# Decoding float64 weights in two VectorE passes instead of four, with one pass more on GpSimd, and chunks two slots earlier

## The chip, the cores and the metric

One core of a Trainium2 chip runs the whole program in one launch. The metric is device time in microseconds, from launch to end; a lower time is better. The profile records one execution of the program, engine by engine.

## The reference

Three layers follow each other: an attention with a threshold, a first feed-forward mixture with a rational activation, and a second mixture of 8 experts with one expert per token. The part that matters here is the middle one, which takes 2304 tokens of width 512 to width 2048 and back:

```python
h = x @ w_in                      # (2304, 512) @ (512, 2048)
P = a[0] + a[1] * h + a[2] * h2 + a[3] * h3
Q = 1.0 + np.abs(b[0]) * np.abs(h) + np.abs(b[1]) * h2
g = P / (Q + 1e-06)
return (g @ w_out).astype(np.float32)
```

`w_in` and `w_out` arrive as float64, because a float32 draw is multiplied by a float64 factor. A weight is thus two 32-bit words, and the kernel makes a float32 of them on the chip: the sign and exponent and the upper 20 bits of the mantissa sit in the high word, three more mantissa bits at the top of the low word. Everything later works with a constant power of two that the scale factors remove.

## The kernel before

**Stages.** The attention runs in steps of one 128-row tile, 144 of them, with a tail of 12 more steps in which only the products with V (L429, "PV" below) and the transposes of the result (L221) are left. A second program, `moe1`, is a generator that the attention loop advances once per step from step 112 on. Its unit is the *slot*: slot 32 is the step after the last score tile, slot 43 is the attention's last step, and from slot 44 on `moe1` runs alone. Each engine works through its instructions in the order in which these two programs wrote them.

**Weights come in 32 pieces** of 128x512 weights (16 of `w_in`, 16 of `w_out`), in the order of `STREAM`. A piece is loaded into one of 5 `raw` buffers by a DMA on the SP queue, and the next load is issued when a piece is finished (`load_next`). Decoding a piece takes five instructions. ScalarE writes the absolute value of the high word, read as a float32 (L609, `mag`). VectorE then clamps it (L612), shifts it left by 3 and masks it (L616), ORs in the low word shifted right by 29 (L620) and ORs in the sign (L625). For the first 8 pieces the intermediate `mag` lies in SBUF, and a table of costs (`RATES`, `decode_steps`) spreads their four passes one by one over slots 32 to 45. For the other 24 it lies in one PSUM bank (`acc`, `aux`), and all four passes of a piece stand in one slot: one piece every 1.6 slots, from slot 47 on.

**After decoding**, a `w_in` piece is summed (L767, ScalarE; for pieces 0 to 3 the sum over partitions is a small matmul L776 of its own on TensorE), scaled (L810; piece (0,2) on GpSimd, L808) and split into two float16 halves, `wih` (L811, ScalarE) and `wil` (L812, GpSimd). A `w_out` piece is split in L817 (ScalarE) and L818 (GpSimd).

**Chunks.** The first mixture's work is 96 chunks, one per slot, of 128 hidden units by 384 tokens, from slot `START` = 43 on. Chunk c has 12 matmuls L893 (`emit_in`), and chunk c-5 has its 9 matmuls L963 in the same slot (`emit_out`). Two chunks share one PSUM tile `h`, and there are two such tiles; a *pair* is two chunks. For each pair the activation is a chain across engines. ScalarE: L917, L918, L919. GpSimd: L920. VectorE: L922, L923. ScalarE: logarithm and exponential, L929 and L930, which overwrite `h`. VectorE: L908, L909, L910, the last reader of `h`. Then L944 (ScalarE) and L945 (GpSimd) split the result. In a slot with the second chunk of a pair, VectorE's order is L908, L909, L910 of the pair before, then the decoding passes of that slot, then L922, L923. In the other slots the decoding passes stand between L923 and L908.

## Time and profile before

| | |
|---|---|
| median of 3 runs | 1044.03 us (1043.01 to 1044.04) |
| the profiled execution | 1049.4 us, span 1047.7 us |
| TensorE busy | 940.3 us, 90% |
| VectorE busy | 832.6 us, 79% |
| ScalarE busy | 688.6 us, 66% |
| GpSimd busy | 502.2 us, 48% |
| granted TensorE clock, mean | 0.971 of full speed |

The shares are averages over stages with different limits. The attention ends about 325 us into the span, the chunks of the first mixture run from there to about 784 us, and decoding goes on until 532 us. In the tables, PE is TensorE, PEld its weight loads, DVE VectorE, ACT ScalarE, POOL GpSimd and SP the queue that issues most DMAs; L12 is line 12 of the kernel before.

### The profile page before, as it was taken

Reading aid. Unit: us, or ns where it says so; the run is one execution under the profiler, and the core shown is the slowest. Engines: PE = TensorE matmul, PEld = TensorE weight load, DVE = VectorE, ACT = ScalarE, POOL = GpSimd, SP = SyncE. Lnnn points to the kernel's source line nnn. Section 1 sums busy time; section 2 is a strip of 40 time slices with the busy share of each in tenths; the row PEclk is TensorE's granted clock in tenths of the full one; section 3 lists DMA queues with packets and bytes.
Section 4 is the critical chain, followed back from the end, with each engine's and each line's share of the span. In section 5 each row is a group of like instructions: output and inputs, shape, how many; then the busy total and the mean of one; then the engine's idle time right before and its main releaser. Section 6 shows DMA issues by size and latency. Waiting matters only on the chain. (4 is left out here: it accounts for less than half of the span.)

```text
span 1047.7 us, 20733 instructions
## 1 busy us (share of the span) xinstructions
PE 940.3 (90%) x7899; PEld 686.8 (66%) x7899; DVE 832.6 (79%) x1381; ACT 688.6 (66%) x1017; POOL 502.2 (48%) x485
## 2 busy tenths in 40 slices
PE   8898899999965887977989989998888999999996
PEld 5565566666553555655656666665557899999995
DVE  5887799999996799999868788898984896665552
ACT  5887788888864787786766666665563555555552
POOL 2687789888943546354454444442533022111120
PEclk9999999999986999999999999999999999999998
DMA  9999999999992134133001131214122111111350
GB/s 213 171 206 200 196 190 184 202 182 196 223 204 85 57 101 131 61 97 105 1 1 61 31 91 41 51 41 131 51 61 101 41 50 63 41 41 41 101 142 23
DMA packets 234187, 110.25 MB, mean 105 GB/s; under 512 B 196832, under 2 KB 221408, under 8 KB 234080
## 3 DMA queue, kind: packets, MB, share of 16 engines
q1 hardware_dynamic: 230816, 98.89, 43.7%
q0 software_dynamic: 3120, 9.96, 3.0%
q8 instruction: 64, 1.05, 0.4%
q14 instruction: 43, 0.35, 0.1%
q10 hardware_dynamic: 144, 0.00, 0.0%
HBM read 82.61 MB, written 13.63 MB: 92 GB/s over the span
## 5 line engine op out<-in xcount | busy, mean ns | idle before, releaser
L893 PE MATMUL h<-xT,wih 128*128 128x384 f16 x768 | 194.9, 337 | 48.9 <-DVE s L910 33.3
L401 POOL TENSOR_TENSOR php<-e,php 128x512 f16<-128x512 f32 x144 | 166.3, 1159 | 65.6 <-ACT php L399 61.8
L920 POOL TENSOR_TENSOR t<-t,ah 128x768 f32<-128x768 f32 x48 | 87.7, 1826 | 228.4 <-ACT t L919 213.8
L893 PEld LDWEIGHTS <-wih 128*128 128x128 f16 x768 | 69.8, 100 | 115.8 <-DVE s L910 40.4
L963 PE MATMUL acc<-woh,gh 128*128 128x512 f32 x288 | 126.4, 439 | 4.5 <-ACT part L980 2.0
L893 PE MATMUL h<-xT,wil 128*128 128x384 f16 x384 | 128.9, 336 | 0.5 <-POOL wil L812 0.5
L383 ACT ACTIVATE e<-s,mn 128x576 f32<-128x576 f32 x144 | 107.1, 743 | 30.7 <-DVE mn L382 26.5
L371 PE MATMUL s<-kt,qT 64*128 64x256 f32 (+3 forms) x640 | 117.0, 456 | 5.9 <-DVE mn L388 5.6
L395 DVE SCALAR_TENSOR_TENSOR e<-s,mn,e 128x576 f32<-128x576 f32 x144 | 116.4, 808 | 5.8 <-ACT e L383 5.8
L429 PEld LDWEIGHTS <-pt 128*128 128x128 f16 (+1 forms) x2240 | 80.5, 102 | 57.3 <-issue 54.0
L963 PE MATMUL acc<-wol,gh 128*128 128x512 f32 x288 | 114.6, 398 | 2.6 <-POOL wol L818 2.6
L963 PE MATMUL acc<-woh,gl 128*128 128x512 f32 x288 | 114.4, 397 | 0.0
L382 DVE TENSOR_REDUCE mn<-s 128x1 f32<-128x576 f32 x144 | 107.8, 748 | 7.0 <-PE s L371 6.9
L1659 POOL DMA_INDIRECT out_dram<-os,sidx x19 | 24.5, 1288 | 184.6 <-ACT os L1658 153.9
L399 ACT ACTIVATE php<-e 128x576 f16<-128x576 f32 x144 | 98.6, 685 | 9.6 <-DMA pt<-php 8.0
L429 PE MATMUL xps<-vs__112,pt 128*128 128x65 f16 (+1 forms) x2240 | 94.8, 197 | 0.0
L945 POOL TENSOR_TENSOR gl<-s,gh 128x768 fp32r<-128x768 f32 x48 | 91.2, 1900 | 6.9 <-issue 4.7
L929 ACT ACTIVATE h<-t,co 128x768 f32<-128x768 f32 x48 | 43.4, 904 | 57.0 <-DVE s L923 21.3
L917 ACT ACTIVATE ah<-h,cvs 128x768 f32<-128x768 f32 x48 | 43.2, 900 | 52.8 <-PE h L893 49.6
L963 PEld LDWEIGHTS acc<-woh,gh 128*128 128x128 f32 x288 | 54.8, 190 | 21.1 <-ACT part L980 4.9
L1592 DVE TENSOR_TENSOR wol<-xT,woh 128x1024 fp32r<-128x1024 f32 x45 | 56.8, 1270 | 14.6 <-ACT woh L1591 14.3
L908 DVE SCALAR_TENSOR_TENSOR t<-t,co,h 128x768 f32<-128x768 f32 x48 | 48.5, 1009 | 24.8 <-ACT h L930 13.4
(382 smaller groups left out, 2320.2 us busy)
## 6 DMA issues: line engine op xcount, KB each, us to landing
xT<-in_moe_w_dram SPq DMA_DIRECT2D x80, 512.0 KB
raw<-in_moe_w_in_dram SPq DMA_DIRECT2D x16, 512.0 KB
raw<-in_moe_w_out_dram SPq DMA_DIRECT2D x16, 512.0 KB
yd<-y SPq DMA_DIRECT2D x18, 256.0 KB
raw<-in_k_dram SPq DMA_DIRECT2D x16, 256.0 KB
raw<-in_q_dram SPq DMA_DIRECT2D x16, 256.0 KB
xT<-in_v_dram SPq DMA_DIRECT2D x8, 512.0 KB
part<-part SPq DMA_DIRECT2D x15, 256.0 KB
```

The costliest lines, as they stand in the source:

```text
L371: nc.tensor.matmul(ps[po:po + m, o:o + n], qT[r, g % 2, hh, t, po:po + m], KT[g][r, bb, c:c + n], start=True, stop=True)
L382: nc.vector.tensor_reduce(mn[:, n:n + 1], st[i], axis=AX.X, op=ALU.min)
L383: nc.scalar.activation(e[:, n], st[i], AF.Exp, bias=mn[:, n:n + 1], scale=-1.0)
L395: nc.vector.scalar_tensor_tensor(e[:, n], st.pop(i), mn[:, 2 + n:3 + n], e[:, n], op0=ALU.is_le, op1=ALU.mult)
L399: nc.scalar.activation(hi, e[:, n], AF.Copy)
L401: nc.gpsimd.tensor_tensor(lo[:, b:b + 512], e[:, n, a:a + 512], hi[:, a:a + 512], op=ALU.subtract)
L429: nc.tensor.matmul(x, pt[:, blk, po:po + m], vv[:, par, hh, j, :], start=False, stop=(i % 6 == 5 and n == 13))
L893: nc.tensor.matmul(hb[:, 0:n], w[:, k, fc * P:(fc + 1) * P], xT[:, k, t0:t0 + TR, lo, :], start=(i == 0), stop=(i == 11))
L920: nc.gpsimd.tensor_tensor(t1, t1, ah, op=ALU.mult)
L945: nc.gpsimd.tensor_tensor(gl, s, gh.bitcast(F32), op=ALU.subtract)
L963: nc.tensor.matmul(acc[r, i], g[:, i * P:(i + 1) * P], w, start=first and m == 0, stop=last and m == 2)
L1592: (self.nc.gpsimd if pool else self.nc.vector).tensor_tensor(cut(lo), src, cut(hi).bitcast(F32), op=ALU.subtract)
```

## The change

A piece is decoded by four instructions now, two of them on VectorE. GpSimd rewrites the low word in place (`last_bits`): it reads the words as unsigned integers, multiplies by 2^-29 and limits to 7.25, which leaves the word's top three bits as a small integer. ScalarE multiplies the high word, read as float32, by 2^-112 instead of taking its absolute value (`exponent`). VectorE shifts that left by 3 and ORs in the low word's three bits (`merge`), then ORs in the sign (`sign`). The clamp and the mask are gone.

```diff
-END = 46
-START = 43
+END = 44
+START = 41
-RATES = ((32, 1050), (42, 1150))
-FIRST_PIECES = 8
-DEC_AT = 47
+FIRST_AT = (32, 33, 35, 37, 38, 40, 42, 43)
+SHIFT_AT = (24, 25, 26, 27, 28)
+SHIFT_LEAD = 3
+DEC_AT = 45
 DEC_EVERY = 1.6
...
-    def mag(self, raw, t):
-        self.nc.scalar.activation(t, raw.bitcast(F32)[:, :, 1], AF.Abs)
-    def clamp(self, t, pool=False):
-        (self.nc.gpsimd if pool else self.nc.vector).tensor_scalar(t, t, HI_BITS, LO_BITS, op0=ALU.min, op1=ALU.max)
-    def shift(self, t):
-        t = t.bitcast(I32)
-        self.nc.vector.tensor_scalar(t, t, 3, 0x3FFFFFF8, op0=ALU.logical_shift_left, op1=ALU.bitwise_and)
-    def low(self, raw, t):
+    def last_bits(self, raw):
+        x = raw.bitcast(U32)[:, :, 0]
+        self.nc.gpsimd.tensor_scalar(x, x, 2.0**-29, 7.25, op0=ALU.mult, op1=ALU.min)
+    def exponent(self, raw, t):
+        self.nc.scalar.activation(t, raw.bitcast(F32)[:, :, 1], AF.Copy, scale=SHORTER)
+    def merge(self, raw, t):
         t = t.bitcast(I32)
         self.nc.vector.scalar_tensor_tensor(
-            t, raw[:, :, 0], 29, t, op0=ALU.logical_shift_right, op1=ALU.bitwise_or)
+            t, t, 3, raw[:, :, 0], op0=ALU.logical_shift_left, op1=ALU.bitwise_or)
...
-    begin, end = plan_decode()
-    for key, i, t in decode_steps():
-        steps.setdefault(t, []).append(lambda key=key, i=i: step(key, i))
-    for key in STREAM:
-        at(begin[key] - (MAG_LEAD if key in STREAM[:FIRST_PIECES] else 1), mag, key)
+    end = decode_at()
+    for n, key in enumerate(STREAM):
+        t = end[key]
+        steps.setdefault(t, []).append(lambda key=key: step(key))
+        at(t - (MAG_LEAD if n < len(FIRST_AT) else 1), exponent, key)
+        at(SHIFT_AT[n] if n < len(SHIFT_AT) else t - (MAG_LEAD if n < len(FIRST_AT) else SHIFT_LEAD), last_bits, key)
```

The first 8 pieces are now decoded in the slots of `FIRST_AT`, the last of them in slot 43 instead of 45. Chunks begin in slot 41 instead of 43, so that chunks 0, 1 and 2 are written among the attention's last three steps; the decoding of the other 24 pieces keeps its distance to the chunks, as does everything that is counted from `START`. GpSimd's new pass stands in slots 24 to 28 for pieces 0 to 4, two slots ahead of the VectorE passes for pieces 5 to 7, and three ahead for the rest.

**VectorE, among chunks 2 to 6**, from the L922 and L923 of the second pair. Before (L908 to L910 and L922, L923 are the activation, L612 to L625 the decoding):

```order
L922 SCALAR_TENSOR_TENSOR s<-s,cvs,h 128x768
L923 SCALAR_TENSOR_TENSOR s<-s,cvs,h 128x768
L612 TENSOR_SCALAR acc<-acc 128x512
L616 TENSOR_SCALAR acc<-acc 128x512
L620 SCALAR_TENSOR_TENSOR acc<-raw,acc 128x512
L625 SCALAR_TENSOR_TENSOR mag<-raw,acc 128x512
L908 SCALAR_TENSOR_TENSOR t<-t,co,h 128x768
L909 SCALAR_TENSOR_TENSOR h<-t,h 128x2x384
L910 SCALAR_TENSOR_TENSOR s<-s,co,h 128x768
```

and now (L892, L893 are the former L922, L923; L878 to L880 the former L908 to L910; L598 is `merge` and L603 `sign`):

```order
L892 SCALAR_TENSOR_TENSOR s<-s,cvs,h 128x768
L893 SCALAR_TENSOR_TENSOR s<-s,cvs,h 128x768
L598 SCALAR_TENSOR_TENSOR acc<-acc,raw 128x512
L603 SCALAR_TENSOR_TENSOR mag<-raw,acc 128x512
L878 SCALAR_TENSOR_TENSOR t<-t,co,h 128x768
L879 SCALAR_TENSOR_TENSOR h<-t,h 128x2x384
L880 SCALAR_TENSOR_TENSOR s<-s,co,h 128x768
```

Two of the four passes between L923 and L908 are gone; the same holds between L910 and L922 in the other kind of slot.

**GpSimd, from the attention's last tiles to the second pair of chunks.** Before (L401 and L407 are the attention's, the others as above):

```order
L401 TENSOR_TENSOR php<-e,php 128x512 x2
L407 TENSOR_TENSOR php<-e,php 128x2x64
L812 TENSOR_TENSOR wil<-mag,wih 128x4x128 x2
L920 TENSOR_TENSOR t<-t,ah 128x768
L808 TENSOR_SCALAR mag<-mag,sc 128x512
L812 TENSOR_TENSOR wil<-mag,wih 128x4x128 x2
L920 TENSOR_TENSOR t<-t,ah 128x768
```

and now (L591 is `last_bits`; L382, L388 the former L401, L407; L783 the former L812, L890 L920, L779 L808):

```order
L591 TENSOR_SCALAR raw<-raw 128x512
L382 TENSOR_TENSOR php<-e,php 128x512 x2
L388 TENSOR_TENSOR php<-e,php 128x2x64
L382 TENSOR_TENSOR php<-e,php 128x512 x2
L388 TENSOR_TENSOR php<-e,php 128x2x64
L783 TENSOR_TENSOR wil<-mag,wih 128x4x128 x2
L591 TENSOR_SCALAR raw<-raw 128x512 x3
L890 TENSOR_TENSOR t<-t,ah 128x768
L591 TENSOR_SCALAR raw<-raw 128x512
L779 TENSOR_SCALAR mag<-mag,sc 128x512
L783 TENSOR_TENSOR wil<-mag,wih 128x4x128 x2
L591 TENSOR_SCALAR raw<-raw 128x512
```

The first row is the fifth `last_bits`; four others stand among the four L382 and two L388 just ahead of it, and one now stands between L920 and L808.

**ScalarE, around the first pair of chunks.** Before (L457 copies a transposed attention result out of PSUM):

```order
L457 ACTIVATE xT<-tp 128x3x128 x2
L917 ACTIVATE ah<-h,cvs 128x768
L918 ACTIVATE s<-h,co,cvs 128x768
L919 ACTIVATE t<-ah,co 128x768
L811 ACTIVATE wih<-mag 128x4x128
L810 ACTIVATE mag<-mag,sc 128x512
L811 ACTIVATE wih<-mag 128x4x128
L929 ACTIVATE h<-t,co 128x2x384
```

and now (L887 to L889 are the former L917 to L919, L782 and L781 the former L811 and L810, L438 the former L457, L899 the former L929):

```order
L887 ACTIVATE ah<-h,cvs 128x768
L888 ACTIVATE s<-h,co,cvs 128x768
L889 ACTIVATE t<-ah,co 128x768
L782 ACTIVATE wih<-mag 128x4x128
L781 ACTIVATE mag<-mag,sc 128x512
L782 ACTIVATE wih<-mag 128x4x128
L438 ACTIVATE xT<-tp 128x3x128 x2
L899 ACTIVATE h<-t,co 128x2x384
```

The last two L457 of the attention moved from ahead of the first pair's activation to behind it and behind the splits of pieces (0,2) and (0,3). On TensorE chunk 0 stands ahead of the last two PV steps now, chunk 1 ahead of the last one, and chunk 2 behind the last transposes.

## Rows read from the trace of the kernel before

**Rows 1.** Busy time in two stretches; columns: stretch, length, each engine, clock, DMA.

```profile
420.19:428.31 8.12, 8.12 (x44) 5.51 (x43) 7.47 (x9) 5.84 (x9) 3.13 (x2) 1.00 0.24 67
354.41:524.46 170.05, 145.98 (x728) 96.17 (x727) 155.53 (x231) 127.84 (x185) 86.30 (x55) 0.98 0.25 79
```

**Rows 2.** TensorE's waits from 354.41 to 524.46: us in total, times, longest.

```profile
PE h L893 <- DVE s L910: 19.5, 12, 3.4
PE acc L963 <- ACT part L980: 2.0, 3, 1.0
PE acc L963 <- DVE part L980: 1.5, 2, 1.4
```

**Rows 3.** VectorE's groups from 354.41 to 524.46: count, busy us, mean ns, idle before.

```profile
L612 DVE TENSOR_SCALAR acc<-acc 128x512 f32<-128x512 f32 x22 | 15.2, 693 | 0.2
L616 DVE TENSOR_SCALAR acc<-acc 128x512 int32<-128x512 int32 x21 | 14.7, 699 | 0.7
```

**Rows 4.** VectorE in order of time: start, duration, instruction, idle before it.

```profile
354.05 0.69 DVE L612 TENSOR_SCALAR acc<-acc 128x512 f32<-128x512 f32 x1
...
356.85 1.01 DVE L922 SCALAR_TENSOR_TENSOR s<-s,cvs,h 128x768 f32<-128x768 f32 x1
...
360.83 1.01 DVE L908 SCALAR_TENSOR_TENSOR t<-t,co,h 128x768 f32<-128x768 f32 x1 [1.93 <-ACT h L930]
...
363.81 0.69 DVE L612 TENSOR_SCALAR acc<-acc 128x512 f32<-128x512 f32 x1
```

**Rows 5.** GpSimd's groups over the whole run, shapes apart.

```profile
L945 POOL TENSOR_TENSOR gl<-s,gh 128x768 fp32r<-128x768 f32 x48 | 91.2, 1900 | 6.9 <-issue 4.7 <-ACT gh L944 2.2
L920 POOL TENSOR_TENSOR t<-t,ah 128x768 f32<-128x768 f32 x48 | 87.7, 1826 | 228.4 <-ACT t L919 213.8 <-issue 14.6
...
L818 POOL TENSOR_TENSOR wol<-mag,woh 128x512 fp32r<-128x512 f32 x16 | 20.4, 1285 | 16.4 <-ACT woh L817 8.5 <-DVE part L980 7.9
L812 POOL TENSOR_TENSOR wil<-mag,wih 128x512 f16<-128x512 f32 x16 | 19.4, 1216 | 20.2 <-ACT wih L811 19.6
...
L351 POOL TENSOR_SCALAR xT<-xT,vs 128x256 f32<-128x256 f32 x28 | 13.4, 480 | 0.0
...
L808 POOL TENSOR_SCALAR mag<-mag,sc 128x512 f32<-128x512 f32 x1 | 1.4, 1385 | 0.0
```

**Rows 6.** ScalarE's two split groups, 290 to 560 us.

```profile
L810 ACT ACTIVATE mag<-mag,sc 128x512 f32<-128x512 f32 x15 | 10.6, 708 | 0.8 <-DVE sc L647 0.8
L811 ACT ACTIVATE wih<-mag 128x512 f16<-128x512 f32 x16 | 10.1, 630 | 3.8 <-POOL mag L808 3.3
```

**Rows 7.** TensorE in order of time where the attention ends.

```profile
317.39 0.59 PE L776 MATMUL h<-tot,co 128*128 128x2 f32 x2 [3.13 <-ACT wih L767]
317.84 1.70 PE L429 MATMUL xps<-vs__112,pt 128*128 128x65 f16 x28
...
325.12 0.82 PE L893 MATMUL h<-xT,wih 128*128 128x384 f16 x2
...
336.88 0.82 PE L893 MATMUL h<-xT,wih 128*128 128x384 f16 x2 [6.70 <-ACT wih L811]
```

**Rows 8.** ScalarE in order of time in the same stretch.

```profile
322.51 0.49 ACT L457 ACTIVATE xT<-tp 128x384 f16<-128x384 f32 x1 [4.22 <-PE tp L221]
...
336.19 0.63 ACT L811 ACTIVATE wih<-mag 128x512 f16<-128x512 f32 x1 [3.28 <-POOL mag L808]
```

**Rows 9.** VectorE, and one GpSimd row, in order of time, 313 to 318 us.

```profile
313.39 0.42 DVE L612 TENSOR_SCALAR mag<-mag 128x512 f32<-128x512 f32 x1
313.85 0.43 DVE L616 TENSOR_SCALAR mag<-mag 128x512 int32<-128x512 int32 x1
...
315.04 1.53 DVE L625 SCALAR_TENSOR_TENSOR mag<-raw,mag 128x512 int32<-128x512 int32 x1
314.86 2.71 POOL L812 TENSOR_TENSOR wil<-mag,wih 128x512 f16<-128x512 f32 x2 [13.67 <-ACT wih L811]
```

**Rows 10.** The SP queue: its last transposes of the attention.

```profile
298.21 8.59 SPq L409 DMA_TRANSPOSE pt<-php  x3
```

More of the change, by code (lines that the diff above doesn't have):

```diff
@@ L14 @@
 I32 = mybir.dt.int32
+U32 = mybir.dt.uint32
 AF = mybir.ActivationFunctionType
@@ L58, with decode_at @@
 STREAM = ((0, 0), (0, 1), (0, 2), (0, 3), (1, 0), (1, 1), (1, 2), (1, 3), (0, 4), (0, 5), (0, 6), (0, 7), (1, 4), (1, 5), (1, 6), (1, 7), (0, 8), (0, 9), (0, 10), (0, 11), (1, 8), (1, 9), (0, 12), (0, 13), (1, 10), (1, 11), (0, 14), (0, 15), (1, 12), (1, 13), (1, 14), (1, 15))
-RATES = ((32, 1050), (42, 1150))
-FIRST_PIECES = 8
-DEC_AT = 47
+FIRST_AT = (32, 33, 35, 37, 38, 40, 42, 43)
+SHIFT_AT = (24, 25, 26, 27, 28)
+SHIFT_LEAD = 3
+DEC_AT = 45
 DEC_EVERY = 1.6
-POOL_CLAMP = frozenset()
-CLAMP_LEAD = 1
-def decode_steps():
-    out, t, credit = [], RATES[0][0], RATES[0][1]
-    for key in STREAM[:FIRST_PIECES]:
-        for i, cost in enumerate((335, 335, 602, 602)):
-            if i == 0 and key in POOL_CLAMP:
-                continue
-            while credit < cost:
-                t += 1
-                credit += [r for s, r in RATES if s <= t][-1]
-            credit -= cost
-            out.append((key, i, t))
-    for n, key in enumerate(STREAM[FIRST_PIECES:]):
-        out += [(key, i, DEC_AT + int(DEC_EVERY * n)) for i in range(4)]
-    return out
-def plan_decode():
-    steps = decode_steps()
-    return {k: t for k, i, t in reversed(steps) if i < 2}, {k: t for k, i, t in steps if i == 3}
+def decode_at():
+    n = len(FIRST_AT)
+    return dict(zip(STREAM, FIRST_AT)) | {key: DEC_AT + int(DEC_EVERY * i) for i, key in enumerate(STREAM[n:])}
 GROUPS = (2,) * (NFC // 2)
@@ L585, in attention @@
     ctx.close()
-LO_BITS = 2.0**-15
-HI_BITS = 122879.9921875
+SHORTER = 2.0**-112
+SIGN = -(1 << 31)
 class Decode:
@@ L625, in sign @@
         self.nc.vector.scalar_tensor_tensor(
-            out.bitcast(I32), raw[:, :, 1], -0x40000000, t, op0=ALU.bitwise_and, op1=ALU.bitwise_or)
+            out.bitcast(I32), raw[:, :, 1], SIGN, t, op0=ALU.bitwise_and, op1=ALU.bitwise_or)
 def pow2_clamp(nc, pool, tot, n):
@@ L709, in run @@
     def run(slot):
-        order = (load_next, mag, clamp, sum_in, red_in, clamp_red, split_out, split_in, scale_in)
+        order = (load_next, last_bits, exponent, sum_in, red_in, clamp_red, split_out, split_in, scale_in)
         for f, args in sorted(hooks.pop(slot, ()), key=lambda x: order.index(x[0]) if x[0] in order else -1 - (x[0] in early)):
@@ L728, in load_next, with last_bits, exponent @@
             load(queue.pop(0))
-    def mag(key):
-        t = mag_buf(key[0]) if key in STREAM[:FIRST_PIECES] else aux()
-        dec.mag(raws[key], t)
-        mags[key] = t
-    def clamp(key):
-        dec.clamp(mags[key], True)
+    def last_bits(key):
+        dec.last_bits(raws[key])
+    def exponent(key):
+        mags[key] = mag_buf(key[0]) if key in STREAM[:len(FIRST_AT)] else aux()
+        dec.exponent(raws[key], mags[key])
     aux_b = []
@@ L748, in mag_buf, with step @@
         return p.tile([P, DM], F32, tag="mag", bufs=n, name="mag")
-    def step(key, i):
+    def step(key):
         raw, t = raws[key], mags[key]
-        if i == 0:
-            dec.clamp(t)
-        elif i == 1:
-            dec.shift(t)
-        elif i == 2:
-            dec.low(raw, t)
-        else:
-            if key not in STREAM[:FIRST_PIECES]:
-                mags[key] = mag_buf(key[0])
-            dec.sign(raw, t, mags[key])
-            del raws[key]
-            load_next()
+        dec.merge(raw, t)
+        if key not in STREAM[:len(FIRST_AT)]:
+            mags[key] = mag_buf(key[0])
+        dec.sign(raw, t, mags[key])
+        del raws[key]
+        load_next()
     def sum_in(n):
@@ L820, in moe1 @@
     at(PRE, coefficients)
-    begin, end = plan_decode()
-    for key, i, t in decode_steps():
-        steps.setdefault(t, []).append(lambda key=key, i=i: step(key, i))
-    for key in STREAM:
-        at(begin[key] - (MAG_LEAD if key in STREAM[:FIRST_PIECES] else 1), mag, key)
-        if key in POOL_CLAMP:
-            at(begin[key] - CLAMP_LEAD, clamp, key)
+    end = decode_at()
[4 more added lines that the diff above has]
+        at(SHIFT_AT[n] if n < len(SHIFT_AT) else t - (MAG_LEAD if n < len(FIRST_AT) else SHIFT_LEAD), last_bits, key)
     n = 0
```

## The prediction

> **What bounds the kernel now.** I read the busy time by stretches first, because the whole run's shares mix stages. In chunks 6 to 39, from 354.41 to 524.46 us, VectorE is busy 155.5 of 170.05 us and TensorE 146.0 [rows 1]. 34 chunks in 170.05 us are 5.00 us each. Chunks 19 and 20, in the same stage, run without a gap: 8.12 us for two, TensorE busy throughout at clock 1.00 [rows 1], so TensorE alone needs 4.06 us each, 138.0 us for the 34. The stage therefore loses 32 us. The view of the waits says to whom: TensorE's next chunk waits 19.5 us for VectorE's L910, the last reader of the PSUM tile, and 3.5 us for the copies L980 [rows 2]; the rest of the 32 us is matmuls at a lower clock behind those waits (mean clock 0.98).
>
> VectorE's timeline shows why. It runs in a loop with ScalarE, since logarithm and exponential may start only when L923 has read `h`, and L908 needs them. One turn goes from 354.05 to 363.81 [rows 4]: 2.80 us for a piece's four passes, 3.98 for L922, L923 and the wait of 1.93 for ScalarE, 2.98 for L908 to L910. That is 9.76 us against the 8.12 that TensorE needs for a pair.
>
> The second place is the attention's end. TensorE waits 3.13 us there for a sum of decoded weights and 6.70 us for a split weight ahead of chunk 2 [rows 7].
>
> **The change, part by part.**
>
> *Two passes fewer in the stage.* L612 and L616 fall away, 22 and 21 of them, 15.2 and 14.7 us, with the gaps ahead of them 30.8 us of VectorE [rows 3]. Where the passes stand between L910 and L922 the turn becomes 9.76 - 1.46 (two starts 0.73 apart) = 8.30 us, 0.18 over TensorE's 8.12; 9 of the stage's pieces stand so, 1.6 us. Where they stand between L923 and L908, two passes of about 0.7 fit into the 1.93 us in which VectorE waits for ScalarE anyway, and cost nothing; without that cover they would be 1.4 a piece. So TensorE's 138.0 us become the base, and I add what is late next.
>
> *GpSimd's new pass, p.* The trace has no unsigned pass and none with gaps between the words. The nearest row is L351, the same kind of operation on 256 float columns, 480 ns, so 0.96 us for 512; L808, on 512, took 1.385 once [rows 5]. I take p = 1.0, the pass most like L351, and keep 0.48 (no faster than half the size) and 2.8 (L808 doubled, for conversion and stride) as ends. 22 passes make GpSimd's 86.3 us [rows 1] 108 of some 150: no bound on average. Two turns are crowded: with L945 and L920 (3.73 us), a pair of L812 (2.43), two L818 and one new pass 9.7 us, or one L818 and two new passes 9.4 [rows 5]. That is 1.6 and 1.3 over 8.12, and L920 of the next pair stands behind it: 2.9 us.
>
> *ScalarE* does the same number of passes; one multiplication replaces an absolute value, which I cost at nothing, hidden or not, since both are one activation over 512 columns (0 to 0.1 us each by the 0.63 and 0.71 of [rows 6]). But its 127.8 us [rows 1] are 7.5 a pair, and a pair with two weight splits has 2 x (0.708 + 0.630) = 2.7 [rows 6] where the mean holds 0.8, so 9.4 us, 1.3 over 8.12. There are five such pairs. Half of it should lie beside L922 and L923: 0.7 each, 3.5 us.
>
> *Waits that stay:* 3.5 us for L980 [rows 2]. The stage then takes 138.0 + 1.6 + 2.9 + 3.5 + 3.5 = 149.5 us, **20.5 us less**, at 4.40 a chunk.
>
> *The attention's end.* Pieces 0 to 3 lose eight passes of 0.42 and 0.43 us [rows 9], 3.4 us, so most of the 3.13 us wait for the second sum goes; I take 2.8, since ScalarE's sum still stands behind work on raw data that leaves only after the transposes. The sum's matmul is then at 314.6. Chunks 0 and 1 follow without the transposes between: 0.45 to the PV row, 1.70 for 28 PV matmuls, 5.06 for two chunks (325.12 to 336.88 less 6.70), 0.85 for 14 PV more [rows 7], so chunk 1 ends about 322.7. From there to the split weight of chunk 2 it was 6.70; now GpSimd has one new pass ahead of L808 (1.0), and the attention's last L457, moved behind the splits, waits for L810 and L811 more (0.7 + 0.6), and from L457 to the first chunk behind the transposes it takes 2.61 (322.51 to 325.12) [rows 6 to 8]. Chunk 2 starts at 322.7 + 11.6 = 334.3 instead of 336.88: **2.6 us sooner**. So the two earlier slots buy little, because the transposes now wait where the chunks waited. If the sum's wait stayed whole, it would be -0.2; if the 6.70 vanished, 9.
>
> *GpSimd among the attention's last tiles.* Five passes, 5 us, delay its last part of the attention. The SP queue's transposes behind it are busy until 306.8 [rows 10], and the last PV rows run at 317.84 [rows 7] or, in the new order, about 322: 5 us of delay lie inside that. Without this cover they would be 5 us on the path. The SP queue's own order is the same.
>
> *Sum:* 20.5 + 2.6 = 23.1 us. It is made against the profiled execution, 1049.4 us, 5.4 above the median; taken from the median of 1044.0 it gives **1020.9 us**. With p = 0.48 the 2.9 and the 1.0 shrink, about 1018; with p = 2.8 GpSimd has (86.3 + 61.6) / 17 = 8.7 us per pair, the stage about 157 us with the waits, the end gains 0.8, so about 1030.
>
> **The rivals.**
>
> *ScalarE and GpSimd take VectorE's place in the loop.* At 4.4 us a chunk ScalarE would be busy 85%, VectorE 83% and GpSimd 72%, in three queues that wait for each other in order, and before the change 91% on one of them was the limit. For it speaks that L908's wait for ScalarE is in the loop already [rows 4]; against it that chunks 19 and 20 ran at TensorE's pace with VectorE 92% busy [rows 1]. At 4.6 us a chunk the stage takes 156.4, the gain is 13.7 + 2.6: 1027.7 us.
>
> *TensorE's floor is reached.* The stage takes 138 us: 32.0 + 2.6 less, 1009.4 us. Against it stand the L980 waits [rows 2], which nothing here removes.
>
> *GpSimd blocks VectorE among the first 8 pieces.* L625 took 1.53 us while L812 ran on GpSimd, against 0.69 to 0.70 for a pass where the pieces lie in PSUM [rows 3, 9], although GpSimd is busy half of that stage. The first 8 pieces' 16 passes still read two SBUF tiles, and the attention's last GpSimd work and five new passes run in the same slots. If half of the 16 are hit, 8 x 0.84 = 6.7 us, and with all of it ahead of chunk 2 the end loses 4.1 instead of gaining 2.6: 20.5 - 4.1 = 16.4, 1027.6 us.
> The Trainium skill (SBUF — State Buffer, Who interferes with whom) says that a VectorE instruction with two SBUF inputs and a GpSimd instruction that reads SBUF exclude each other for their whole length, and one with a single SBUF input is left alone; the row of 1.53 us and the PSUM rows agree with it. By it the stage's term stands and the end's is the one in doubt.
>
> *Slower: the new GpSimd pass is far longer than float rows tell.* If the integer form runs in another way than L351, GpSimd becomes the bound: 86.3 + 22 p passes 170.05 us at p = 3.8. At p = 5 the stage takes 196, 26 us more, and chunk 2 comes 1.4 later than before: 1071 us. Nothing in the trace has this form, so nothing excludes it; that every float row lies within 1.9 us speaks against it.
>
> *The change doesn't do what it says:* the loop keeps 5.00 us a chunk, because VectorE's passes were only filling waits for something else. The end's -0.2 to 2.6 is left, 1041 to 1044 us. The turn of 9.76 us in [rows 4], full but for 1.93, speaks against it.
>
> **How the numbers follow.** My forecast gets 0.57, ScalarE and GpSimd in the loop 0.18, the blocked first pieces 0.10, TensorE's floor 0.08, the long GpSimd pass 0.04, no effect 0.03. A measurement of this kernel can tell about 0.2%, 2 us, from no change. The first four cases are faster by more: 0.93; no effect counts as same, 0.03; slower 0.04. The range goes from the floor case, 1009, to loop and blocking together (13.7 - 4.1 = 9.6 us less), 1034.4, so 1035; that covers the bounds of p as well and leaves out the last two cases and little more.
>
> **What would show it.** Right: the stage of chunks 6 to 39 near 149.5 us with VectorE about 125 busy; TensorE's wait for L910's successor well under 10 us; the new pass near 1.0 us; chunk 2 about 334. Wrong: a pass beyond 2.8 us; TensorE's waits as long as before but with ScalarE or GpSimd as releaser; first-piece passes at 1.4 us; chunk 2 later than 337, with a wait on the transposes ahead of it.

## The result and the profile after

The changed kernel takes **1031.33 us** (median of 4 runs, 1030.23 to 1032.74) against 1044.03 for the kernel before (4 runs, 1043.01 to 1044.63): a ratio of 0.988, 95% interval 0.9863 to 0.9897, 12.7 us less. The forecast was 1020.9, 23.1 less; its range, 1009 to 1035, holds the result. Run again later beside the experiments, the same kernel took 1031.01 against 1045.45 (ratio 0.9862, 0.9829 to 0.9895).

| | before | after |
|---|---|---|
| the profiled execution | 1049.4 us, span 1047.7 | 1030.73 us, span 1029.0 |
| TensorE busy | 940.3 us | 934.9 us |
| VectorE busy | 832.6 us | 796.2 us |
| ScalarE busy | 688.6 us | 688.7 us |
| GpSimd busy | 502.2 us | 566.7 us |

**The stage of chunks 6 to 39.** The chunks are found again by TensorE's first L863 (the former L893) of each. Busy time by stretches, columns as in [rows 1]; first two chunks at TensorE's pace, then the stage:

```profile
409.20:417.31 8.11, 8.11 (x42) 5.52 (x43) 6.48 (x8) 6.40 (x10) 6.92 (x4) 1.00 0.39 124
...
354.04:507.10 153.06, 142.28 (x727) 95.57 (x727) 131.56 (x189) 127.90 (x186) 129.93 (x77) 0.99 0.27 88
```

The stage takes 153.06 us where it took 170.05. The pace of two chunks without a gap is the same, 8.11 us. VectorE went from 155.5 busy to 131.6, GpSimd from 86.3 to 129.9. The waits in the same stretch, TensorE's and VectorE's (us in total, times, longest):

```profile
PE h L863 <- DVE s L880: 10.1, 9, 1.9
...
DVE t L878 <- POOL gl L915: 9.4, 5, 3.0
DVE t L878 <- ACT h L900: 7.8, 4, 3.0
```

TensorE's wait for the last reader of `h` is half of the 19.5 us of [rows 2], and the 3.5 us for the copies are gone. VectorE is still the one waited for, but it waits more itself: 17.2 us, for GpSimd and ScalarE, where it was 9.8 us, for ScalarE alone. The groups of the new instructions in that stretch:

```profile
L598 DVE SCALAR_TENSOR_TENSOR acc<-acc,raw 128x512 int32<-128x512 int32 x22 | 15.2, 693 | 0.4 <-ACT acc L594 0.4
L603 DVE SCALAR_TENSOR_TENSOR mag<-raw,acc 128x512 int32<-128x512 int32 x21 | 14.4, 687 | 0.7
...
L591 POOL TENSOR_SCALAR raw<-raw 128x512 uint32<-128x512 uint32 x22 | 44.1, 2006 | 1.8
```

Two VectorE passes of the old length are left; GpSimd's new one takes 2.0 us, twice what I took.

**The attention's end.** GpSimd in order of time (start, duration, idle before in brackets); L382 and L388 are the attention's:

```profile
291.75 2.00 POOL L591 TENSOR_SCALAR raw<-raw 128x512 uint32<-128x512 uint32 x1
...
295.07 2.43 POOL L591 TENSOR_SCALAR raw<-raw 128x512 uint32<-128x512 uint32 x1
...
299.60 1.96 POOL L591 TENSOR_SCALAR raw<-raw 128x512 uint32<-128x512 uint32 x1
...
306.47 0.43 POOL L388 TENSOR_TENSOR php<-e,php 128x128 f16<-128x128 f32 x1
```

ScalarE's first sum and TensorE, in order of time:

```profile
306.93 0.63 ACT L738 ACTIVATE wih<-mag 128x512 f16<-128x512 f32 x1 [10.34 <-POOL php L388]
```

```profile
308.69 0.59 PE L747 MATMUL h<-tot,co 128*128 128x2 f32 x2 [11.91 <-ACT wih L738]
...
317.72 0.59 PE L747 MATMUL h<-tot,co 128*128 128x2 f32 x2 [0.41 <-ACT wih L738]
...
332.54 1.54 PE L202 MATMUL tp<-ident,xf 128*64 128x128 f32 x10 [6.17 <-DVE xf L421]
336.33 1.55 PE L202 MATMUL tp<-ident,xf 128*64 128x128 f32 x12 [2.25 <-DVE xT L444]
337.81 0.82 PE L863 MATMUL h<-xT,wih 128*128 128x384 f16 x2
```

GpSimd's last attention row ends at 306.90; before, that row (there L407) ended at 301.19. Only then does the first sum begin, and TensorE stands for 11.91 us (before 4.63, and for VectorE's decoding, not for GpSimd). The three rows of before, of GpSimd, ScalarE and TensorE:

```profile
300.58 0.61 POOL L407 TENSOR_TENSOR php<-e,php 128x128 f16<-128x128 f32 x1
302.68 0.63 ACT L767 ACTIVATE wih<-mag 128x512 f16<-128x512 f32 x1 [1.74 <-DVE mag L625]
305.96 0.59 PE L776 MATMUL h<-tot,co 128*128 128x2 f32 x2 [4.63 <-ACT wih L767]
```

The second sum's matmul comes at 317.72, as in [rows 7] (317.39) and not at the 314.6 that I had. Chunk 2 starts at 337.81, later than the 336.88 of before; forecast was 334.3.

These times hide a part of the loss, because the attention does not reach the same place at the same time in every execution. VectorE's reduction of score tile 134 (the tiles are counted from 0) stands 8 us ahead of GpSimd's first new pass, and nothing that the change moved stands ahead of it. Before, then after:

```profile
280.07 0.75 DVE L382 TENSOR_REDUCE mn<-s 128x1 f32<-128x576 f32 x1
276.64 0.75 DVE L363 TENSOR_REDUCE mn<-s 128x1 f32<-128x576 f32 x1
```

So the profile of the change had come 3.4 us ahead by chance. From this row, chunk 2 starts 61.17 us on where it was 56.81, and chunk 6 starts 77.40 us on where it was 74.34: the attention's end lost 4.4 us up to chunk 2 and 3.1 us up to chunk 6. The second profiles of both kernels, below, give 3.8 and 2.5.

So three questions went to the chip: whether two VectorE passes fewer carry the gain, what GpSimd's 2.0 us cost and come from, and what the attention's end lost by.

### The profile page after: what moved, and what is told of

The parts are those of the page before. It is cut to its first block, busy times and chain, and to the rows that moved or that the text cites. A ratio compares the mean times of both kernels' runs of the same rounds, so it can differ in the third digit from the quotient of the medians.

```text
span 1029.0 us, 20719 instructions
## 1 busy us (share of the span) xinstructions
PE 934.9 (91%) x7899; PEld 687.3 (67%) x7899; DVE 796.2 (77%) x1317; ACT 688.7 (67%) x1017; POOL 566.7 (55%) x517
## 5 line engine op out<-in xcount | busy, mean ns | idle before, releaser
L863 PE MATMUL h<-xT,wih 128*128 128x384 f16 x768 | 192.2, 333 | 31.1 <-DVE s L880 23.7
L382 POOL TENSOR_TENSOR php<-e,php 128x512 f16<-128x512 f32 x144 | 166.8, 1163 | 60.1 <-ACT php L380 59.2
L890 POOL TENSOR_TENSOR t<-t,ah 128x768 f32<-128x768 f32 x48 | 87.9, 1831 | 176.3 <-ACT t L889 155.3
L863 PEld LDWEIGHTS <-wih 128*128 128x128 f16 x768 | 68.9, 99 | 96.3 <-DVE s L880 31.8
L863 PE MATMUL h<-xT,wil 128*128 128x384 f16 x384 | 127.3, 331 | 0.0
L1629 POOL DMA_INDIRECT out_dram<-os,sidx x19 | 23.8, 1251 | 186.6 <-ACT os L1628 155.5
L915 POOL TENSOR_TENSOR gl<-s,gh 128x768 fp32r<-128x768 f32 x48 | 91.3, 1903 | 5.4 <-issue 4.7
L899 ACT ACTIVATE h<-t,co 128x768 f32<-128x768 f32 x48 | 43.4, 905 | 55.3 <-POOL t L890 21.9
L887 ACT ACTIVATE ah<-h,cvs 128x768 f32<-128x768 f32 x48 | 43.3, 902 | 51.0 <-PE h L863 46.4
L878 DVE SCALAR_TENSOR_TENSOR t<-t,co,h 128x768 f32<-128x768 f32 x48 | 48.5, 1011 | 35.6 <-POOL gl L915 19.8
L591 POOL TENSOR_SCALAR raw<-raw 128x512 uint32<-128x512 uint32 x32 | 65.6, 2051 | 2.7
```

What stands on the lines that cost most here:

```text
L382: nc.gpsimd.tensor_tensor(lo[:, b:b + 512], e[:, n, a:a + 512], hi[:, a:a + 512], op=ALU.subtract)
L591: self.nc.gpsimd.tensor_scalar(x, x, 2.0**-29, 7.25, op0=ALU.mult, op1=ALU.min)
L863: nc.tensor.matmul(hb[:, 0:n], w[:, k, fc * P:(fc + 1) * P], xT[:, k, t0:t0 + TR, lo, :], start=(i == 0), stop=(i == 11))
L890: nc.gpsimd.tensor_tensor(t1, t1, ah, op=ALU.mult)
L915: nc.gpsimd.tensor_tensor(gl, s, gh.bitcast(F32), op=ALU.subtract)
```

## The experiments

Each has its own runs of the kernel before beside it. This table collects the profiles: when chunk 2 and chunk 6 start, how long chunks 6 to 39 take (us), and the timed median with its ratio to before. Chunk 2 is given from the span's start and from tile 134; the second is the one to compare, except where passes are spread, since four of the five stand ahead of tile 134 there. The stage repeats within 0.7 us wherever GpSimd's pass is the same; with the old decoding the three profiles lie 1.5 us apart.

| kernel | chunk 2 | from tile 134 | chunk 6 | chunks 6 to 39 | median | ratio (95%) |
|---|---|---|---|---|---|---|
| before | 336.88 | 56.81 | 354.41 | 170.05 | 1044.0 to 1045.7 | 1 |
| before, again | 335.32 | 56.95 | 352.78 | 168.60 | one execution, 1049.62 | |
| four passes, new slots | 337.38 | 57.57 | 354.62 | 168.99 | 1044.3 | 0.9993 (0.997 to 1.0015) |
| the change | 337.81 | 61.17 | 354.04 | 153.06 | 1031.33 | 0.988 (0.9863 to 0.9897) |
| the change, again | 338.26 | 60.75 | 354.39 | 153.00 | 1031.01 | 0.9862 (0.9829 to 0.9895) |
| sums to a bank of their own | 339.30 | 60.57 | 355.68 | 153.05 | 1031.82 | 0.9868 (0.9841 to 0.9896) |
| first passes spread | 335.52 | 56.43 | 351.25 | 153.16 | 1028.41 | 0.9833 (0.9805 to 0.986) |
| slots not moved | 335.67 | 55.73 | 353.73 | 152.52 | 1029.29 | 0.9834 (0.9805 to 0.9863) |
| both of these | 332.06 | 52.55 | 350.13 | 152.86 | 1027.54 | 0.9826 (0.9799 to 0.9854) |
| spread, and own bank | 331.70 | 54.02 | 347.92 | 153.02 | 1025.30 | 0.9809 (0.9779 to 0.984) |
| no GpSimd pass | 333.48 | 51.69 | 350.06 | 150.14 | 1020.23 | 0.9755 (0.9728 to 0.9781) |
| second GpSimd pass | 339.20 | 60.97 | 355.99 | 177.31 | 1058.17 | 1.0124 (1.0085 to 1.0162) |
| multiply and add | 329.60 | 51.85 | 345.64 | 154.74 | 1027.28 | 0.9828 (0.9798 to 0.9858) |
| multiply and add, spread, own bank | 327.46 | 49.36 | 343.81 | 154.69 | 1025.34 | 0.9811 (0.9773 to 0.9849) |

**The kernel before, once more**, for a second profile.

> The kernel before, unchanged, for a second profile. The first profile's execution took 1049.4 us, 5.4 more than the median. Theory 'profile': that execution was unusual, and this one lies within 1.5 us of 1044, with the missing 4 to 6 us to be found in one place (the attention, or chunks 6 to 43). Rival: profiled executions of this kernel are always about 5 us longer, and this one takes 1048 to 1050 again.

Its profiled execution took 1049.62 us, the rival's number, while 11 timed runs of it beside had a median of 1045.69 (1041.97 to 1051.49). So an execution of the kernel before scatters by some 5 us to either side, and both of its profiles fell near the upper end. Two cannot tell a rule from chance; the profiled executions of the other kernels lie from 3.7 us below their medians to 4.1 above, so chance is enough. The second profile differs in the parts too: its stage takes 168.60 us, 1.5 less than the first, so that the change's gain in the stage is 15.6 to 17.0 us.

**The change, once more**, timed beside the experiments that follow it.

> The changed kernel, unchanged, for a second profile and a time beside the others of this call. Theory 'loop': the gain comes from the turns of chunks 6 to 43 alone, which take 166 to 168 us against 185 to 187 before; chunk 6 starts at 352 to 356 as before, and the time is 1029 to 1033. Rival 'lucky profile': the stage's gain in the two profiles is larger than usual, and the stage takes 170 us or more here.

1031.01 us, 14.4 under the 1045.45 beside it; the stage is the first profile's within 0.1 us.

**Four passes in the new slots**: the old decoding under the new order.

```diff
     def last_bits(self, raw):
-        x = raw.bitcast(U32)[:, :, 0]
-        self.nc.gpsimd.tensor_scalar(x, x, 2.0**-29, 7.25, op0=ALU.mult, op1=ALU.min)
+        pass
...
+        self.nc.vector.tensor_scalar(t, t, 122879.9921875, 2.0**-15, op0=ALU.min, op1=ALU.max)
+        self.nc.vector.tensor_scalar(t, t, 3, 0x3FFFFFF8, op0=ALU.logical_shift_left, op1=ALU.bitwise_and)
...
```

> The changed kernel's slots (first pieces at FIRST_AT, chunks from 41) with the old decoding: absolute value on ScalarE, four VectorE passes per piece, no pass on GpSimd. Theory 'loop': the four passes are what made the turns long, so chunks 6 to 43 take 183 to 190 us again, and the time is 1041 to 1050, like before. Rival 'slots': the new slots carry the gain, and it takes 1031 to 1036.

1044.3 us, no difference. The stage by stretches, and TensorE's longest wait in it:

```profile
354.62:523.61 168.99, 146.37 (x726) 95.90 (x726) 155.77 (x231) 128.25 (x185) 86.50 (x55) 0.98 0.25 80
```

```profile
PE h L864 <- DVE s L881: 17.0, 10, 3.4
```

With the two passes back, VectorE is at 155.8 busy and TensorE's wait is back at 17.0. The whole gain is the new decoding's, two passes fewer on VectorE with one more on GpSimd; the order alone gives none.

**The sums to a bank of their own.** ScalarE's sum of a piece writes a by-product that nobody reads. It goes to `wih`, whose memory the attention used up to then. Here it goes to a PSUM bank.

```diff
+        hi = bank(1).rearrange("p (k f) -> p k f", k=4) if n < 4 else wih[:, :, n * P:(n + 1) * P]
         nc.scalar.activation(
-            wih[:, :, n * P:(n + 1) * P], mags[0, n].rearrange("p (k f) -> p k f", k=4), AF.Abs,
+            hi, mags[0, n].rearrange("p (k f) -> p k f", k=4), AF.Abs,
```

> The changed kernel, with one edit: the absolute values that the sums of pieces 0 to 3 write as a by-product go to a PSUM bank instead of wih, whose memory was the attention's. Theory 'memory': the first sum no longer waits for GpSimd's last attention pass (10.3 us of idle ScalarE, 11.9 us of idle TensorE in the profile), it comes 4 to 8 us sooner, and the kernel is 2 to 5 us faster than the changed one (1026 to 1029). Rival 'decode': the sum waits for the decoding itself or for something behind it, and the time stays within 1 us of 1031.

1031.82 us: nothing gained. The time is the rival's, though its reason, the decoding, is not what the rows show. TensorE in order of time, then ScalarE:

```profile
302.06 0.38 PE L748 MATMUL h<-tot,co 128*128 128x2 f32 x2 [1.45 <-ACT acc L739]
310.74 0.48 PE L400 MATMUL xps<-tiny 128*128 128x390 bf16 x1 [6.99 <-DVE xf L421]
318.58 0.58 PE L748 MATMUL h<-tot,co 128*128 128x2 f32 x2 [3.85 <-ACT acc L739]
```

```profile
309.48 0.63 ACT L783 ACTIVATE wih<-mag 128x512 f16<-128x512 f32 x1 [3.87 <-POOL php L388]
...
317.26 0.65 ACT L594 ACTIVATE mag<-raw 128x512 f32<-128x512 f32 x1 [3.25 <-DMA raw<-in_moe_w_out_dram]
```

The first wait is gone (1.45 instead of 11.91), so the shared memory did cause it. But the split weights go to `wih` too and wait for the same GpSimd row, and the next raw data comes after the transposes that also wait for it. The wait moved from one of GpSimd's dependents to the others.

**The first five passes spread** over the attention's slots 6 to 23.

```diff
-SHIFT_AT = (24, 25, 26, 27, 28)
+SHIFT_AT = (6, 10, 14, 18, 23)
```

> The changed kernel with GpSimd's first five passes in slots 6, 10, 14, 18 and 23 instead of 24 to 28. Theory 'crowding': five passes of 2.0 us in five consecutive attention steps delay GpSimd's last attention pass by about 6 us; spread out, most of them fit into its idle time, the last pass comes 3 to 6 us sooner and the kernel takes 1026 to 1029. Rival 'no slack': GpSimd is busy 85% there, the attention is slowed by the same 10 us of passes wherever they stand, and the time stays at 1030 to 1033.

1028.41 us. GpSimd's last attention row ends at 304.95, 2.0 us sooner (the first theory had 3 to 6), and TensorE's wait for the first sum falls to 4.36; the time is the first theory's:

```profile
304.08 0.87 POOL L388 TENSOR_TENSOR php<-e,php 128x128 f16<-128x128 f32 x1
```

```profile
306.74 0.59 PE L747 MATMUL h<-tot,co 128*128 128x2 f32 x2 [4.36 <-ACT wih L738]
```

**The two slots not moved.**

```diff
-END = 44
-START = 41
+END = 46
+START = 43
...
-DEC_AT = 45
+DEC_AT = 47
```

> The changed kernel with chunks from slot 43, END 46 and DEC_AT 47, as before; the decoding and the first pieces' slots are the changed kernel's. Theory 'decode pays': the two earlier slots are worth nothing, since chunk 2 waits for the attention's last transposes there; this takes 1029 to 1033. Rival 'start pays': the two slots are part of the gain, about two chunks' 8 us, and this takes 1037 to 1041.

1029.29 us; its interval and that of the change overlap. TensorE in order of time:

```profile
326.56 1.54 PE L202 MATMUL tp<-ident,xf 128*64 128x128 f32 x10 [1.29 <-DVE xf L421]
329.32 1.55 PE L202 MATMUL tp<-ident,xf 128*64 128x128 f32 x12 [1.22 <-DVE xT L444]
345.44 0.82 PE L863 MATMUL h<-xT,wih 128*128 128x384 f16 x2 [5.71 <-DVE s L880]
```

The waits ahead of the last transposes, 6.17 and 2.25 in the change, are 1.29 and 1.22 here; in their place stands one of 5.71 a few chunks later. The earlier slots buy nothing: chunks 0 and 1 then stand ahead of the transposes, but the VectorE work of their pair stands ahead of L421, on which the transposes wait. From tile 134, chunk 6 comes after 73.79 us here and after 77.40 and 76.88 in the two profiles of the change, so the earlier slots may even cost a little.

**Both edits**, first passes spread and slots not moved.

> The changed kernel with both single edits that were no slower: GpSimd's first five passes spread over slots 6 to 23, and chunks from slot 43 as before. Theory 'order at the end': the two edits act in different places (GpSimd's last attention pass; the transposes behind the first pair), so their gains of about 3 and 1 to 2 us add, 1024 to 1028. Rival 'one wait': both only move the same wait, and it takes 1028 to 1030 like each alone.

1027.54 us: inside the first theory's range, but not to be told from the spread passes alone.

**No GpSimd pass at all.** The decoding ORs in a zero instead, so the three lowest bits of every weight of this mixture are left out.

```diff
-        x = raw.bitcast(U32)[:, :, 0]
-        self.nc.gpsimd.tensor_scalar(x, x, 2.0**-29, 7.25, op0=ALU.mult, op1=ALU.min)
+        pass
...
-            t, t, 3, raw[:, :, 0], op0=ALU.logical_shift_left, op1=ALU.bitwise_or)
+            t, t, 3, self.zero, op0=ALU.logical_shift_left, op1=ALU.bitwise_or)
```

> The changed kernel without GpSimd's pass; merge ORs in a zero instead, so the three lowest mantissa bits of every weight of the first mixture are left out. Theory 'GpSimd limits now': 32 passes of 2.0 us hold up L890 in the crowded turns and the attention's end; without them chunks 6 to 43 take 155 to 161 us, the first sum comes 4 to 6 us sooner and the kernel takes 1016 to 1023. Rival 'ScalarE limits now': the stage stays at 163 to 167 us and the time at 1025 to 1030, the attention's end alone being gained.

1020.23 us, 10.8 less than the change: this bounds what the pass can cost. The time is the first theory's. The stage is not: with chunks 40 to 42 it takes 163.9 us, the rival's 163 to 167, so GpSimd's pass is not what mainly limits it. Without the pass chunks 6 to 39 take 150.14 us, 2.9 less, and chunk 6 starts 4.0 to 4.3 sooner. The attention of this profile had run late, though, before the place of the pass: tile 134 came at 281.79 (276.64 in the change), and 2.4 us of this lie between tiles 118 and 130, where the granted clock had a mean of 0.93, and 1.00 in the change. From tile 134, chunk 6 comes after 68.27 us, 8.6 to 9.1 sooner than in the change. So the long pass costs about 9 us at the attention's end and 3 us in the stage.

**A second GpSimd pass** behind the new one for 24 pieces, in three forms by turns.

```diff
+        if n >= 0 and n % 3 == 0:
+            x = raw.bitcast(U32)[:, :, 0]
+            nc.gpsimd.tensor_scalar(x, x, 1.0, 7.25, op0=ALU.mult, op1=ALU.min)
+        if n >= 0 and n % 3 == 1:
+            y = raw.bitcast(F32)[:, :, 0]
+            nc.gpsimd.tensor_scalar(y, y, 1.0, 7.25, op0=ALU.mult, op1=ALU.min)
+        if n >= 0 and n % 3 == 2:
+            z = raw.bitcast(U32).rearrange("p n t -> p (n t)")[:, 0:DM]
+            nc.gpsimd.tensor_scalar(z, z, 1.0, 4294967040.0, op0=ALU.mult, op1=ALU.min)
```

> The 24 later pieces get a second GpSimd pass behind the new one, in three forms, 8 pieces each: the same pass over unsigned words with gaps of one word (multiply by 1, limit 7.25), the same in place over float32 with the same gaps, and an unsigned pass over 512 words side by side (multiply by 1, limit 4294967040, which rounds the low bits of some high words away). Theory 1, the pass takes 2.0 us because it converts integers: the float form takes 0.7 to 1.0 us and the unsigned form without gaps 2.0. Theory 2, it is the gaps: the float form takes 2.0, the form without gaps 0.7 to 1.0. If it is both, each lies between, near 1.4. Time: GpSimd was busy 141 of 166.6 us in the stage of chunks 6 to 43; some 22 passes more of 1.0 to 2.0 us make that 163 to 185, so if GpSimd's load sets the stage it takes 175 to 195 us and the whole run 1040 to 1055; if the load does not matter while the queue's order is kept, 167 and 1031.

Both theories of the pass fell; the stage with chunks 40 to 42, 190.9 us, is the one expected if GpSimd's load sets it, and the time lies 3 us above its range. GpSimd's groups over the whole run:

```profile
L717 POOL TENSOR_SCALAR raw<-raw 128x512 f32<-128x512 f32 x8 | 16.0, 2001 | 0.7
L714 POOL TENSOR_SCALAR raw<-raw 128x512 uint32<-128x512 uint32 x8 | 16.0, 2000 | 0.7
L720 POOL TENSOR_SCALAR raw<-raw 128x512 uint32<-128x512 uint32 x8 | 15.4, 1922 | 0.7
```

Float32 with gaps takes 2.00 us, unsigned words without gaps 1.92. What the three share, and L351 of [rows 5] does not, is the second operation: a limit, where L351 adds a zero. The stage takes 177.31 us:

```profile
355.99:533.30 177.31, 151.11 (x727) 98.89 (x726) 136.51 (x189) 126.83 (x185) 170.99 (x98) 0.94 0.24 76
```

GpSimd is busy 171.0 of it and is the bound here. In the change it is busy 129.9 of 153.06 and is not, as the next run shows.

**Multiply and add.** The same pass with an addition of zero as second operation.

```diff
-        self.nc.gpsimd.tensor_scalar(x, x, 2.0**-29, 7.25, op0=ALU.mult, op1=ALU.min)
+        self.nc.gpsimd.tensor_scalar(x, x, 7.49 * 2.0**-32, 0.0, op0=ALU.mult, op1=ALU.add)
```

> GpSimd's new pass multiplies by 7.49 x 2^-32 and adds 0 in place of multiplying by 2^-29 and limiting to 7.25 (the three lowest bits are rounded a little differently); words, gaps and place are the same. L332, a multiply and add on 256 float columns, takes 480 ns, and the single L779, on 512, took 695. Theory 1, the pass is long because its second operation is a limit: 0.7 to 1.0 us here; then GpSimd has some 22 us less to do in the stage of chunks 6 to 43, this is the kernel that the prediction had priced, and it takes 1019 to 1023 us, chunk 2 starts near 334 and the stage takes 161 to 164 us. Theory 2, unsigned words or the gaps between them make it long, each alone enough: 2.0 us, and 1031 us as for the change itself.

Theory 1 holds for the pass. GpSimd's group in the stage, and the stage by stretches:

```profile
L591 POOL TENSOR_SCALAR raw<-raw 128x512 uint32<-128x512 uint32 x22 | 14.6, 664 | 1.8
```

```profile
345.64:500.38 154.74, 142.49 (x727) 95.64 (x727) 135.56 (x189) 128.15 (x186) 102.88 (x78) 0.99 0.27 87
```

The pass falls from 2.0 to 0.66 us, where only the second operation and the constants differ. Chunk 2 starts at 329.60, 8.2 us sooner than in the change; from tile 134 it takes 51.85 us, as without any pass (51.69). But the stage is not shorter: 154.74 us, 1.7 longer, although GpSimd does 27 us less; with chunks 40 to 42 it is 168.3, not the 161 to 164 expected. And the time, 1027.28 us, misses the 1019 to 1023 expected. Chunk 43 starts 6.7 us sooner than in the change (513.91 against 520.64); from there to the end of the span it is 511.0 us against 508.4, where all profiles lie between 505 and 511.

What grew in the stage is VectorE, from 131.6 to 135.6 us. VectorE, then GpSimd, in order of time in that kernel; the VectorE rows are the handful of instructions on two or four numbers that make the scale factors of two `w_in` pieces:

```profile
491.31 0.15 DVE L609 TENSOR_SCALAR t<-h 128x2 f32<-128x2 f32 x1
491.49 0.71 DVE L617 TENSOR_SCALAR g<-t 128x2 int32<-128x2 int32 x1
492.12 0.16 DVE L621 TENSOR_SCALAR g<-t 128x2 int32<-128x2 int32 x1
492.24 1.76 DVE L625 TENSOR_SCALAR sc<-g 128x2 f32<-128x2 f32 x1
...
494.11 0.62 DVE L764 TENSOR_TENSOR cvs<-sc,vs 128x4 f32<-128x4 f32 x1
...
494.84 2.53 DVE L769 TENSOR_SCALAR cvs<-cvs,co 128x4 f32<-128x4 f32 x2
```

```profile
490.34 1.84 POOL L890 TENSOR_TENSOR t<-t,ah 128x768 f32<-128x768 f32 x1 [5.13 <-ACT t L889]
492.14 1.84 POOL L915 TENSOR_TENSOR gl<-s,gh 128x768 fp32r<-128x768 f32 x1
494.06 0.67 POOL L591 TENSOR_SCALAR raw<-raw 128x512 uint32<-128x512 uint32 x1
494.81 2.53 POOL L789 TENSOR_TENSOR wol<-mag,woh 128x512 fp32r<-128x512 f32 x2
```

Each long row ends with a GpSimd row: L617 at 492.20 (L890 at 492.18), L625 at 494.00 (L915 at 493.98), L764 at 494.73 (L591 at 494.73), L769 at 497.37 (L789 at 497.34). Between two GpSimd rows the same kind takes 0.16 us. VectorE's L878, on which the pair hangs, stands behind them. Beside the long pass of the change it is otherwise; VectorE, then GpSimd, in that profile:

```profile
376.49 0.64 DVE L764 TENSOR_TENSOR cvs<-sc,vs 128x4 f32<-128x4 f32 x1
377.17 0.16 DVE L767 TENSOR_TENSOR cvs<-cvs 128x4 f32<-128x4 f32 x1
```

```profile
376.45 4.10 POOL L591 TENSOR_SCALAR raw<-raw 128x512 uint32<-128x512 uint32 x2
```

In chunks 6 to 42 of the change 30 of these small rows (without L609, which reads PSUM) lie wholly inside one long pass: 25 take 0.16 to 0.23 us, five 0.61 to 0.66, and the pass runs on behind them; one more, of 0.64 us, ends with its pass. With the short pass they meet other GpSimd rows instead. Three profiles beside each other, in us: the stage, VectorE's wait in it for GpSimd's L915, and by how much the small rows that last over 0.3 us exceed 0.16 us each:

| pass | stage | wait for L915 | small rows |
|---|---|---|---|
| none | 150.14 | 4.7 | 11.2 |
| multiply and add, 0.66 us | 154.74 | 4.8 | 14.3 |
| multiply and limit, 2.0 us | 153.06 | 9.4 | 11.0 |

The long pass holds VectorE up through L915; the short pass does not, but with it the small rows take longer. Both are read from the profiles; no run took either away alone.

**All three edits that helped, or might, together.**

> Three edits together: the pass as multiply and add, its first five copies in slots 6, 10, 14, 18 and 23, and the sums' by-product in a PSUM bank. Theory 1, the two gains at the attention's end are the same one: with a pass of 0.68 us chunk 2 started at 329.6 already, and the early passes no longer hold GpSimd's last attention row up, so the other two edits add nothing: 1026 to 1028 us, chunk 2 near 329. Theory 2, the memory shared between the sums and the attention still costs there (TensorE's wait of 5.9 us ahead of the first sum's matmul): 2 to 4 us less, 1023 to 1025, chunk 2 near 327.

1025.34 us. Chunk 2 starts at 327.46, 2.1 sooner than with the multiply and add alone, and TensorE waits 2.14 instead of 5.93 for the first sum, so the shared memory did still cost something; the time lies on the edge between the two theories.

**Passes spread, and the sums' own bank**, with the long pass.

> The first five GpSimd passes stand in slots 6, 10, 14, 18 and 23, and the sums of pieces 0 to 3 write their by-product to a PSUM bank instead of wih. If the wait for the attention's last GpSimd row is all that the early passes cost, moving them takes it away already and the second edit adds nothing: 1028 us, as with the passes moved alone, chunk 2 near 335.5. If the memory that the sums share with the attention still holds TensorE up there (the wait of 4.4 us that was left for the sum's matmul), 2 to 4 us less, 1024 to 1026, chunk 2 near 332.

1025.30 us, chunk 2 at 331.70: the second theory, since the bank that gave nothing alone gives 3.8 us at chunk 2 once GpSimd's last row is early (2.4 us from tile 134). This version and the one above beat both kernels, by 19 to 20 us against before and about 6 against the change, and are not to be told from each other.

## Why the prediction was off by half

**The mechanism held for the gain, not for what is left.** The stage was bounded by VectorE's turn, and the two passes in it carry the gain: with them, 1044.3; without, 1031. But of the four signs of being right none was met in full: VectorE is busy 131.6 us and not near 125, TensorE waits 10.1 us for L880 and not well under 10, the pass takes 2.0 us and chunk 2 comes at 337.8. One sign of being wrong came: chunk 2 later than 337, with a wait on the transposes ahead of it. The stage's 153.06 us, 4.50 a chunk, lie as near to the rival "ScalarE and GpSimd take VectorE's place" (156.4) as to the forecast's 149.5, and VectorE's 17.2 us of waits for these two are what that rival describes; it came in part. The floor case (138 us) did not come.

**The account of the 10.4 us that are missing**, on the two profiles: the sum promised 23.1. The stage gave 17.0 instead of 20.5 (3.5 missing). From tile 134 to chunk 6 it became 3.1 longer instead of 2.6 shorter (5.7 missing). The attention up to tile 134 came 3.4 sooner, which is luck. Chunks 40 to 42, which I had not counted, gave 3.1 more (16.64 to 13.54). Behind chunk 43 it became 1.8 longer (506.6 to 508.4). That makes 18.6, the 18.7 between the spans but for rounding. The last 6.0 lie between the profiled executions and the medians: before 5.4 above, after 0.6 below. From tile 134 to chunk 43 alone the two pairs of profiles give 17.0 and 16.2 us, where the medians show 12.7 and 14.4; no run shows where the 2 to 4 us between them go.

**The step that failed: "GpSimd among the attention's last tiles."** I hid five passes of 1.0 us behind the SP queue's transposes and said that without this cover they would be on the path. The cover was not there. At about 2.0 us each, the five delayed GpSimd's last attention row by 9.1 us from tile 134 on, not by 5, and those that wait for that row are the transposes themselves and, through memory that changes hands, ScalarE's first sum. The SP queue's waits ahead of its last three transposes, in the change and then before:

```profile
SPq L390 <- POOL raw L591: 6.5, 1, 6.5
SPq L390 <- POOL php L388: 4.5, 1, 4.5
```

```profile
SPq L409 <- POOL php L401: 2.5, 1, 2.5
```

The queue that I read as busy until 306.8 in [rows 10] had stood waiting for GpSimd in part already. With "the second sum's matmul at 314.6" (it came at 317.72; from tile 134, 3.8 us later than before instead of 2.8 sooner) falls "2.6 us sooner". The stretch from chunk 1's end to chunk 2 was nearly right, 12.4 us against 11.6, and by the chain that was forecast. GpSimd, then ScalarE:

```profile
330.29 2.29 POOL L591 TENSOR_SCALAR raw<-raw 128x512 uint32<-128x512 uint32 x1
```

```profile
333.40 0.63 ACT L782 ACTIVATE wih<-mag 128x512 f16<-128x512 f32 x1 [5.08 <-POOL mag L779]
...
335.21 0.47 ACT L438 ACTIVATE xT<-tp 128x384 f16<-128x384 f32 x1
```

The pass ahead of L779 takes 2.29 us where 1.0 was counted, and from L438 to chunk 2 it is 2.60 us, as forecast. The 6.17 us for which TensorE waits for L421 end earlier: the transposes behind that wait are done at 334.08, and ScalarE is free for L438 only at 335.21.

**The term that was mis-sized: p.** I took 1.0 us by L351 and it is 2.0, inside the ends of 0.48 and 2.8. I chose the nearest row by its size and number of operations; the row has another second operation, and that decides. Where p mattered was not where I priced it. In the stage the pass costs 2.9 us at p = 2.0, the size that I had given to 1.0, and 4.6 at 0.66, so that "2.9 us" does not grow with p there. From tile 134 to chunk 2 no pass and the short pass are alike (51.7 and 51.9 us), and the long one takes 61.2. With the short pass, chunk 2 came 4.7 us ahead of my 334.3.

**The stage's 3.5 us** are not p's either: without any pass the stage takes 150.14, and the sum without its 2.9 for GpSimd is 146.6, again 3.5 apart. On TensorE's side the sum had 138.0 us busy and 11.5 lost; the profile has 142.28 busy and 10.8 idle. The losses come out in total, though not one by one: my term for the copies (3.5) is gone from the waits, and TensorE's wait for L880 is 10.1. What is missing is 4.3 us by which TensorE is busy beyond 4.06 a chunk. Before, that was 8.0 us; I saw it behind the waits, kept 11.5 us of waits and put it at nothing. I had laid it to the lower clock, which explains the smaller part: the second profile of before has a mean clock of 1.00 in the stage and TensorE busy 143.44. The rest stays open. The small scale instructions are a part of VectorE's delay: those on two or four numbers that last over 0.3 us exceed 0.16 us each by 5.7 us in chunks 6 to 42 before and by 11.0 in the change, and by 11.2 without the pass, so it is not the pass that doubled them. That they end with GpSimd rows is read from the trace; no run took them away, so how much of the stage is theirs stays open.

**The rivals.** "GpSimd blocks VectorE among the first 8 pieces" had the right place but not the price: of the 14 decoding rows that the trace holds between 294.96 and 331.79 us, only two lasted over 1.1 us (1.53 and 1.33), against 8 supposed; with four more of about 1.0 they add 3.0 us over 0.69 each, not 6.7. That 1027.6 lay nearer to the result than the forecast is luck. The slower rival needed p = 3.8; the second pass shows it in kind: GpSimd bound, 1058.17 us.

**Still open:** without any GpSimd pass the median is 7.0 us below that with multiply and add. The stage accounts for 4.6 of them (150.14 against 154.74). In the two profiles chunk 43 starts at the same time (513.95 and 513.91) only because the attention without the pass had come 4.0 us later to tile 134 (281.79 and 277.75). The other 2.4 are within what lies behind chunk 43, which scatters by 6 us between executions and was not taken apart.

## What to carry to other kernels

Hiding an added pass behind a transfer means nothing until it is clear that the transfer does not itself start behind that pass; follow every dependent of the last row that is delayed, also those by memory that changes hands. Take an unknown instruction's price from a row with the same operations, not only with the same size. And when one profile stands for a kernel whose executions scatter by 5 us, say the gain against that profile and discount it against the median; and compare two profiles from a row that the change cannot have moved, not from the start of the span.
